# Spreading VectorE's four folds of a batch's values over four half steps

## The chip, the cores and the metric

The kernel runs on one core of a Trainium2 chip. Its time is the device time of one execution in microseconds (us); shorter is better. The core has five engines with one instruction queue each, which run in program order and wait for one another through semaphores: TensorE (PE in the profile, with its weight loads as PEld), VectorE (DVE), ScalarE (ACT), GpSimd (POOL) and SyncE (SP), which here only issues transfers.

## The reference

Attention over pooled keys and values, then a mixture of experts in which every token goes to one expert. The change lies in the pooling of `v`.

```
# q, k, v: (8 batches, 8 heads, 576 tokens, 64)
k_p = k.reshape(B, H, 72, 8, D).mean(axis=3)
v_p = v.reshape(B, H, 72, 8, D).mean(axis=3)
scores = scale * np.matmul(q, k_p.transpose(0, 1, 3, 2))
attn = softmax(scores)
x = np.matmul(attn, v_p)              # to (4608 tokens, 512)
...
logits = x @ w_gate                   # 8 experts
e_idx = np.argmax(logits, axis=1)
out[mask] = gate_w * sigmoid(x @ w_output_gate)[e] * (relu(x[mask] @ w1[e]) @ w2[e])
```

## The kernel before

The program has two parts. `attention_and_routing` does the attention and writes each token's row, sorted by expert, to a table in memory; `experts` then multiplies the sorted rows. The change lies in the first part, whose order is written out by hand.

The 4608 tokens are 36 tiles of 128. The main loop runs over tiles `i` and, within a tile, over two halves of the heads, `a` = 0 (three heads in `values`) and 1 (five). One pass is called a **half step** here and numbered `i` or `i + 0.5`. In half step `i + 0.5 a` the program emits, in this order: TensorE's `scores` of tile `i` (L276); `transpose_p` of tile `i - 2` (L300, evacuated by ScalarE at L301); VectorE's `peak` of tile `i` (L282, the maximum `m`); two units of queued work; TensorE's `values` of tile `i - 3` (L310) with a reciprocal on VectorE (L327); one unit of queued work; ScalarE's `softmax` of tile `i` (L288); VectorE's `normalise` of tile `i - 3` (L333, which empties the accumulator into `xg`); one unit of queued work. There is one accumulator `p_y[a]` for each half of the heads, so `values` of the next tile must wait until `normalise` has emptied it.

The queued work is a list of generators. `work(n)` takes the first whose hold has run out and advances it by one `yield`; the number yielded is the hold in half steps. Two kinds stand there. `route(g)`, appended for each group of four tiles, is some 15 small VectorE operations (L349 to L398) that choose the expert and end in `where`, the table rows, after which GpSimd scatters the group's four tiles (L441). `pooled(b)`, inserted at the head, is the four **folds** (L228) of batch `b`.

Pooling a batch's values goes in stages. SyncE loads `v` of a batch into `vt` (L189), five chunks of 128 rows, one buffer for all batches. GpSimd halves each chunk (L224; `halve_v(b, 0)` is chunks 0 to 2, `halve_v(b, 1)` chunks 3 and 4). VectorE folds what is left twice for each part: **fold 1** (128x384) and **fold 2** (128x192, into the tile `vp`) for chunks 0 to 2, which need the first three halvings, then **fold 3** (128x256) and **fold 4** (128x128, into `vp`) for chunks 3 and 4. `turn_v` (L248) transposes `vp` on TensorE, and `place_v` copies it on ScalarE. `vt` may be loaded again only after the last fold.

A plan says what is emitted at the end of which half step: what stands at `at(s, ...)` is emitted at the end of half step `s + 0.5`. Batch `b` is first used by the scores of half step `f`: 4.5, 9, 13.5, 18, 22.5, 27 and 31.5 for `b` = 1 to 7. Before, the halvings come at the ends of half steps `f - 2.5` and `f - 2`, the four folds all in half step `f - 1`, and at the end of half step `f` come `turn_v` of the batch and the next batch's load of `v`. GpSimd also pools the keys (L202, nine operations a batch).

Of the kernel before, what the change touches and what calls it, by code (L numbers as in the profile page):

```python
# [91 lines left out]
def attention_and_routing(ctx, tc, sh, qT, kT, v, wg, wst, xs):  # L92
# [133 lines left out]
    def pool_v(b, a, n):  # L226
        to = vt[:, part_v(a), 0:n] if n > D else pooled_rows(b)[:, part_v(a)]
        nc.vector.tensor_tensor(to, vt[:, part_v(a), 0:n], vt[:, part_v(a), n:2 * n], op=ALU.add)  # L228
# [293 lines left out]
    plan, queue = {}, []  # L522

    def at(step, f, *args):
        plan.setdefault(step, []).append((f, args))

    def pooled(b):
        for a in range(2):
            for n in (2 * D, D):
                pool_v(b, a, n)  # L530
                yield 0

    tick = [0]

# [14 lines left out]
    for b in range(1, B):  # L549
        f = S * b // P + 0.5 * (b % 2)  # L550
        at(f - 8.5, load_k, b)
        at(max(f - 5, 0), load_v, b)
        at(f - 4.5, load_q, b)
        for i, part in enumerate([(w, c, c + 1) for c in range(4) for w in (4, 2)] + [(1, 0, 4)]):
            step = f - 5.5 + 0.5 * (i // 2)
            at(step if step != -0.5 else 0, pool_k, b, nc.gpsimd, *part)
        at(max(f - 2.5, 1.5), scale_k, b)
        at(f - 3, halve_v, b, 0)
        at(f - 2.5, halve_v, b, 1)
        at(f - 2, lambda b: queue.insert(0, [pooled(b), 0, -1]), b)  # L560
        for c in range(3):
            at(f - 0.5 + 0.5 * c, place_v, b, c)
        at(f - 0.5, turn_v, b)
        at(f + 1.5, gate_v, b)
# [809 lines left out]
def program():  # L1374
# [12 lines left out]
    with ExitStack() as st:  # L1387
# [31 lines left out]
        with tile.TileContext(nc) as tc:  # L1419
            with ExitStack() as ctx, tc.manual_schedule():  # L1420
                attention_and_routing(ctx, tc, sh, qT, kT, v, wg, wst, xs)
# [32 lines left out]
```

## Time and profile before

| what | value |
|---|---|
| median of 3 runs | 602.16 us (602.12 to 604.27) |
| profiled execution, its own time | 602.74 us |
| profiled execution, span of its instructions | 600.8 us |
| TensorE busy | 572.1 us, 95% of the span |
| VectorE, ScalarE, GpSimd busy | 363.7, 256.4 and 223.9 us |

The profile is one execution; its span leaves out 1.94 us around the instructions. Times of rows count from the span's start. Attention fills about the first 150 us, the experts the rest.

### The profile page before, as it was taken

To read this page: it belongs to the slowest core of one execution; us is meant where nothing else is said; L and a number is where in the kernel's file an instruction comes from. 1 tells how busy PE (TensorE), PEld (TensorE's weight loads), DVE (VectorE), ACT (ScalarE), POOL (GpSimd) and SP (SyncE) were. 2 spreads that over 40 slices of the span, in tenths; PEclk is the share of its full clock that TensorE was granted. 3 is DMA by queue.
4 is the path that set the end of the run, shared out by engine and by line. 5 is a ranking of instruction groups with operands and counts; after the bars stand their busy time and mean duration, and the time that the engine had idled before them with its cause. 6 is when DMAs were issued, how large, how long until landed. Compare 5 with 4: busy or idle time off the path is not lost.

```text
span 600.8 us, 11852 instructions
## 1 busy us (share of the span) xinstructions
PE 572.1 (95%) x3427; PEld 518.9 (86%) x3428; DVE 363.7 (61%) x892; ACT 256.4 (43%) x709; POOL 223.9 (37%) x331
## 2 busy tenths in 40 slices
PE   2899999999999999999999999999999999999996
PEld 2798898888888989898989898898998898989895
DVE  6788899988978725698575324664253832232323
ACT  2888988788525304266344121441140430202120
POOL 2849789851526322224224131232202422213131
PEclk9999999999999999999999999999999999999999
DMA  9767888975557433589656213363033112010111
GB/s 338 292 239 289 351 304 314 373 292 163 189 203 193 164 101 116 146 238 327 207 192 202 62 38 88 124 211 64 37 133 99 48 31 69 17 52 19 35 36 35
DMA packets 44683, 96.60 MB, mean 161 GB/s; under 512 B 5515, under 2 KB 28475, under 8 KB 41664
## 3 DMA queue, kind: packets, MB, share of 16 engines
q1 hardware_dynamic: 29328, 48.95, 25.4%
q10 hardware_dynamic: 7488, 27.27, 13.6%
q0 software_dynamic: 7792, 19.61, 9.2%
q14 instruction: 56, 0.46, 0.2%
q8 instruction: 19, 0.31, 0.2%
HBM read 76.36 MB, written 22.91 MB: 165 GB/s over the span
## 4 chain that ended last, share of the span: by engine, by line
PE 68%; issue 2%; DVEq 0%; DVE 0%; POOL 0%; POOLq 0%
PE p_h L1031 34%; PE p_y L1012 33%; PE p_y L665 1%; POOL out L1353 0%; DVE rows L1204 0%; DVEq L1207 0%; PE p_y L1068 0%; DVE q_even L1230 0%; DVEq L793 0%; POOLq L1318 0%; DVEq L767 0%; DVEq L1237 0%; DVEq L926 0%; DVEq L853 0%; DVEq L785 0%
## 5 line engine op out<-in xcount | busy, mean ns | idle before, releaser
L1113 ACT ACTIVATE ht<-p_h 128x384 fp32r<-128x384 f32 (+1 forms) x104 | 46.8, 450 | 246.4 <-PE p_h L1031 219.1
L1353 POOL DMA_INDIRECT out<-rows,dst x41 | 42.2, 1030 | 210.4 <-DVE rows L1204 207.3
L1031 PE MATMUL p_h<-xt,w1b 128*128 128x384 f32 (+1 forms) x736 | 115.5, 317 | 2.0 <-issue 2.0
L1031 PEld LDWEIGHTS p_h<-xt,w1b 128*128 128x128 f32 x736 | 114.4, 189 | 3.3 <-issue 2.9
L1215 DVE SCALAR_TENSOR_TENSOR ht<-p_h,ht 128x384 fp32r<-128x384 f32 (+1 forms) x104 | 52.3, 504 | 100.0 <-ACT ht L1113 90.6
L1012 PE MATMUL p_y<-w2b,ht 128*128 128x512 f32 x480 | 110.4, 390 | 0.0
L1012 PEld LDWEIGHTS p_y<-w2b,ht 128*128 128x128 f32 x480 | 89.8, 188 | 18.4
L1031 PEld LDWEIGHTS p_h<-xt,w1a 128*128 128x128 f32 x640 | 92.7, 190 | 2.6 <-DVE q_even L1230 1.2
L1031 PE MATMUL p_h<-xt,w1a 128*128 128x256 f32 (+1 forms) x640 | 93.7, 306 | 1.2 <-DVE q_even L1230 1.0
L1012 PE MATMUL p_y<-w2a,ht 128*128 128x512 f32 x408 | 94.0, 390 | 0.0
L1012 PEld LDWEIGHTS p_y<-w2a,ht 128*128 128x128 f32 x408 | 76.3, 188 | 15.6
L1204 DVE TENSOR_SCALAR rows<-p_y,sc 128x512 f32<-128x512 f32 x41 | 30.1, 742 | 84.3 <-PE p_y L1012 75.9
L288 ACT ACTIVATE p<-p_h,m 128x72 f32<-128x72 f32 x288 | 69.8, 347 | 16.3 <-DVE m L282 14.3
L310 PE MATMUL p_y<-vbd,pT 128*128 128x162 f32 (+3 forms) x400 | 68.7, 320 | 6.1 <-DVE xg L333 4.4
L1328 POOL DMA_INDIRECT rows<-xs,src x51 | 57.6, 1129 | 25.0 <-POOL src L1324 13.5
L310 PEld LDWEIGHTS p_y<-vbd,pT 128*128 128x128 f32 (+1 forms) x400 | 54.2, 179 | 11.1 <-issue 5.7
L441 POOL DMA_INDIRECT xs<-xg,where x36 | 36.0, 1000 | 38.4 <-DVE grec L327 17.2
L202 POOL TENSOR_TENSOR kq<-kq 128x288 f32<-128x288 f32 (+1 forms) x63 | 42.2, 675 | 17.4 <-DMA kq<-kT 14.4
L276 PE MATMUL p_h<-kbd,q_even 128*128 128x144 f32 (+1 forms) x160 | 28.7, 307 | 11.5 <-DMA q_even<-qT 8.8
L333 DVE TENSOR_TENSOR xg<-p_y,grec 128x240 f32<-128x240 f32 x72 | 35.2, 489 | 1.4
L276 PEld LDWEIGHTS p_h<-kbd,q_even 128*128 128x128 f32 (+1 forms) x160 | 22.8, 191 | 13.6 <-issue 9.5
L1168 DVE STREAM_TRANSPOSE turned<-rows 128x512 f32<-128x512 f32 x51 | 32.4, 686 | 3.2 <-DMA rows<-xs 1.5
(170 smaller groups left out, 657.7 us busy)
## 6 DMA issues: line engine op xcount, KB each, us to landing
stage<-wst ACTq DMA_DIRECT2D x52, 512.0 KB
rows<-v SPq DMA_DIRECT2D x8, 1280.0 KB
kq<-kT SPq DMA_DIRECT2D x7, 1152.0 KB
rows<-xs SPq DMA_DIRECT2D x36, 192.0 KB
stage<-wst SPq DMA_DIRECT2D x12, 512.0 KB, 5.0
kq<-qT SPq DMA_DIRECT2D x4, 1152.0 KB
q_even<-qT SPq DMA_DIRECT2D x3, 1152.0 KB, 8.5
rows<-xs SPq DMA_DIRECT2D x20, 128.0 KB
```

What stands on the lines that cost most here:

```text
L202: eng.tensor_tensor(k[:, :, 0:w], k[:, :, 0:w], k[:, :, w:2 * w], op=ALU.add)
L276: nc.tensor.matmul(s[r0:r0 + n, 144 * c:144 * c + 144], q_t[b][:, 2 * a + c, s0:s0 + n], kbd[b % 2][:, 2 * a + c, :], start=True, stop=True)
L288: nc.scalar.activation(pt[i % 3][:, o:o + KEYS], sv[:, h], AF.Exp, bias=m[:, h:h + 1])
L310: nc.tensor.matmul(av[r0:r0 + n, COLS * h:COLS * (h + n_heads)], pT[:, c, r0:r0 + n], vbd[b % 2][:, slot:slot + n_heads].rearrange("p h f ...
L333: nc.vector.tensor_tensor(xg[g][:, j, 0:LEAD + DM].rearrange("p (f h) -> p f h", h=H)[:, :, hs], avv[:, :, 0:GATE + D].rearrange("p h f -> ...
L441: ins = nc.gpsimd.indirect_dma_start(out=whole_rows(xs), out_offset=bass.IndirectOffsetOnAxis(ap=where, axis=0), in_=x.bitcast(I32), in_of ...
L1012: i = mm(to, ht[:, h, f, P * k:P * k + P], w[:, part, o:o + DM], start=(f == 0 and part == 0 and h == 0), stop=(f == 7 and h == 1))
L1031: i = mm(to, w[:, part, o:o + P], x, start=(d == 0 and k == 0), stop=(d == 3 and k == len(terms) - 1))
L1113: act(ht[:, 0, f, 0:size * P], p_h[f % DEEP][:, 0:size * P], AF.Relu).then_inc(q["hh"], 1)
L1215: nc.vector.scalar_tensor_tensor(ht[:, 1, f, 0:n], src, 0.0, ht[:, 0, f, 0:n].bitcast(F32), op0=ALU.max, op1=ALU.subtract).then_inc(q["hl" ...
L1328: nc.gpsimd.indirect_dma_start(out=xm[:, k].bitcast(I32), out_offset=None, in_=xs, in_offset=bass.IndirectOffsetOnAxis(ap=src[:, k:k + 1], ...
L1353: nc.gpsimd.indirect_dma_start(out=out, out_offset=bass.IndirectOffsetOnAxis(ap=dst[:, k:k + 1], axis=0), in_=yb[2 if k == size - 1 else k ...
```

## The change

`pooled(b)` yields a hold of 1 where it yielded 0, so that at most one fold is taken in a half step, and it is put into the queue half a step sooner. Fold 1 moves from half step `f - 1` to `f - 1.5`, fold 2 stays in `f - 1`, fold 3 moves to `f - 0.5` and fold 4 to `f`. The number of instructions on VectorE and what each computes stay as they are.

```diff
     def pooled(b):
         for a in range(2):
             for n in (2 * D, D):
                 pool_v(b, a, n)
-                yield 0
+                yield 1
...
         at(f - 3, halve_v, b, 0)
         at(f - 2.5, halve_v, b, 1)
-        at(f - 2, lambda b: queue.insert(0, [pooled(b), 0, -1]), b)
+        at(f - 2.5, lambda b: queue.insert(0, [pooled(b), 0, -1]), b)
```

VectorE's rows around the folds of batch 1, in the program before (`m_0` and `m_1` are the maxima of a tile's two halves; L228 with `rows` as output is fold 1 or 3, with `vp` fold 2 or 4):

```order
53 L282 TENSOR_REDUCE m_0_287<-p_h 128x4
54 L327 RECIPROCAL grec_293<-p_y 128x3
55 L333 TENSOR_TENSOR xg_291<-p_y,grec_293 128x80x3
56 L282 TENSOR_REDUCE m_1_307<-p_h 128x4
57 L228 TENSOR_TENSOR rows<-rows 128x3x128
58 L228 TENSOR_TENSOR vp_310<-rows 128x192
59 L327 RECIPROCAL grec_293<-p_y 128x5
60 L228 TENSOR_TENSOR rows<-rows 128x2x128
61 L333 TENSOR_TENSOR xg_291<-p_y,grec_293 128x80x5
62 L228 TENSOR_TENSOR vp_310<-rows 128x128
63 L282 TENSOR_REDUCE m_0_333<-p_h 128x4
```

The four folds stand between two maxima. In the changed program the same stretch begins with fold 1 ahead of the first reciprocal:

```order
53 L282 TENSOR_REDUCE m_0_287<-p_h 128x4
54 L228 TENSOR_TENSOR rows<-rows 128x3x128
55 L327 RECIPROCAL grec_294<-p_y 128x3
56 L333 TENSOR_TENSOR xg_292<-p_y,grec_294 128x80x3
57 L282 TENSOR_REDUCE m_1_308<-p_h 128x4
58 L228 TENSOR_TENSOR vp_310<-rows 128x192
59 L327 RECIPROCAL grec_294<-p_y 128x5
60 L333 TENSOR_TENSOR xg_292<-p_y,grec_294 128x80x5
```

and goes on with folds 3 and 4:

```order
61 L282 TENSOR_REDUCE m_0_331<-p_h 128x4
62 L228 TENSOR_TENSOR rows<-rows 128x2x128
63 L327 RECIPROCAL grec_294<-p_y 128x3
64 L333 TENSOR_TENSOR xg_292<-p_y,grec_294 128x80x3
65 L282 TENSOR_REDUCE m_1_353<-p_h 128x4
66 L228 TENSOR_TENSOR vp_310<-rows 128x128
67 L327 RECIPROCAL grec_294<-p_y 128x5
```

Each fold now stands right behind a maximum; fold 4 is two maxima later than it was. On TensorE the transposes of batch 1's `vp` stand where they stood, and the second of them waits for VectorE (the number behind an engine's name names its semaphore). The rows of the changed program, behind the last `values` of half step 4.5:

```order
47 L310 MATMUL p_y<-vbd_69,pT_282 128x162 [waits DVE_49,Activation_49]
48 L310 MATMUL p_y<-vbd_69,pT_282 128x243
49 L310 MATMUL p_y<-vbd_69,pT_282 128x162
50 L248 MATMUL vtr_367<-ident,vp_310 128x128 [waits PE_49]
51 L248 MATMUL vtr_367<-ident,vp_310 128x128 [waits DVE_49]
52 L248 MATMUL vtr_367<-ident,vp_310 64x128
```

These read the same before; what moved is the fold that row 51 waits for. On GpSimd the scatters of a group move with the routing that shares the queue with the folds. Around the halvings of batch 3, the program before (`where_580` is of group 0, `where_838` of group 1):

```order
69 L441 DMA xs<-xg_291,where_580 39296x528
70 L202 TENSOR_TENSOR kq<-kq 128x4x72 [waits Pool_49]
71 L322 IOTA xg_719 128x4x16
72 L224 TENSOR_TENSOR rows<-rows 128x256 [waits DMAHW6_49]
73 L224 TENSOR_TENSOR rows<-rows 128x256 x4
74 L202 TENSOR_TENSOR kq<-kq 128x288 [waits DMAHW0_49,Activation_49]
75 L202 TENSOR_TENSOR kq<-kq 128x144 [waits Pool_49]
76 L441 DMA xs<-xg_489,where_838 39296x528 [waits DVE_49]
```

and the changed program (`where_603` is of group 0, `where_820` of group 1):

```order
69 L202 TENSOR_TENSOR kq<-kq 128x4x72 [waits Pool_49]
70 L322 IOTA xg_717 128x4x16
71 L441 DMA xs<-xg_292,where_603 39296x528
72 L224 TENSOR_TENSOR rows<-rows 128x256 [waits DMAHW6_49]
73 L224 TENSOR_TENSOR rows<-rows 128x256 x4
74 L441 DMA xs<-xg_489,where_820 39296x528 [waits DVE_49]
75 L202 TENSOR_TENSOR kq<-kq 128x288 [waits DMAHW0_49,Activation_49]
76 L202 TENSOR_TENSOR kq<-kq 128x144 [waits Pool_49]
```

Group 1's first scatter, and VectorE's routing that it waits for, now stand ahead of two of batch 4's key operations instead of behind them.

## Rows read from the trace of the kernel before

**Rows 1.** The page's head and its busy times: us, share of the span, instructions.

```profile
span 600.8 us, 11852 instructions
...
PE 572.1 (95%) x3427; PEld 518.9 (86%) x3428; DVE 363.7 (61%) x892; ACT 256.4 (43%) x709; POOL 223.9 (37%) x331
```

**Rows 2.** Stretches in attention and in the experts: busy us of each engine, clock, DMA.

```profile
60.00:80.00 20.00, 19.52 (x151) 18.15 (x152) 17.84 (x72) 17.14 (x69) 14.68 (x20) 1.00 0.76 295
...
300.00:400.00 100.00, 100.00 (x581) 91.47 (x580) 51.55 (x77) 31.86 (x56) 24.23 (x35) 1.00 0.43 127
```

**Rows 3.** TensorE's waits from 15 to 240 us: us in total, times, longest.

```profile
PE p_y L310 <- DVE xg L333: 4.4, 6, 1.5
```

**Rows 4.** VectorE's waits, the same stretch.

```profile
DVE rows L228 <- POOL rows L224: 4.4, 4, 1.6
```

**Rows 5.** VectorE in order of time, batch 1: start, us, instruction [idle before, releaser].

```profile
23.83 1.07 DVE L228 TENSOR_TENSOR rows<-rows 128x384 f32<-128x384 f32 x1 [1.60 <-POOL rows L224]
24.93 0.77 DVE L228 TENSOR_TENSOR vp<-rows 128x192 f32<-128x192 f32 x1
25.63 0.18 DVE L327 RECIPROCAL grec<-p_y 128x5 f32<-128x5 f32 x1
25.73 0.38 DVE L228 TENSOR_TENSOR rows<-rows 128x256 f32<-128x256 f32 x1
...
26.52 0.61 DVE L228 TENSOR_TENSOR vp<-rows 128x128 f32<-128x128 f32 x1
27.05 0.45 DVE L282 TENSOR_REDUCE m<-p_h 128x4 f32<-128x288 f32 x1
27.42 0.16 DVE L327 RECIPROCAL grec<-p_y 128x3 f32<-128x3 f32 x1
...
27.94 0.45 DVE L282 TENSOR_REDUCE m<-p_h 128x4 f32<-128x288 f32 x1
28.30 0.18 DVE L327 RECIPROCAL grec<-p_y 128x5 f32<-128x5 f32 x1
...
29.01 0.45 DVE L282 TENSOR_REDUCE m<-p_h 128x4 f32<-128x288 f32 x1
```

**Rows 6.** TensorE in order of time, batches 1 and 4.

```profile
23.81 0.72 PE L310 MATMUL p_y<-vbd,pT 128*128 128x162 f32 x4
...
26.75 1.20 PE L310 MATMUL p_y<-vbd,pT 128*128 128x162 f32 x6 [1.10 <-DVE xg L333]
27.79 0.49 PE L248 MATMUL vtr<-ident,vp 128*128 128x128 f32 x3
...
75.31 1.13 PE L310 MATMUL p_y<-vbd,pT 128*128 128x162 f32 x6
...
77.57 0.49 PE L248 MATMUL vtr<-ident,vp 128*128 128x128 f32 x3
```

**Rows 7.** GpSimd in order of time, batches 3 and 4.

```profile
54.60 3.77 POOL L224 TENSOR_TENSOR rows<-rows 128x256 f32<-128x256 f32 x5
58.34 1.60 POOL L202 TENSOR_TENSOR kq<-kq 128x288 f32<-128x288 f32 x2
62.44 0.99 POOL L441 DMA_INDIRECT xs<-xg,where  x1 [2.50 <-DVE grec L327]
...
72.06 3.80 POOL L224 TENSOR_TENSOR rows<-rows 128x256 f32<-128x256 f32 x5
```

**Rows 8.** VectorE in order of time: batch 2's fold 1, and around batch 4's.

```profile
40.64 0.54 DVE L228 TENSOR_TENSOR rows<-rows 128x384 f32<-128x384 f32 x1
...
71.76 0.46 DVE L282 TENSOR_REDUCE m<-p_h 128x4 f32<-128x288 f32 x1
...
74.58 0.70 DVE L228 TENSOR_TENSOR rows<-rows 128x384 f32<-128x384 f32 x1
```

**Rows 9.** SyncE's waits: us in total, times, longest.

```profile
SPq L189 <- DVE vp L228: 72.2, 6, 16.4
```

**Rows 10.** A stretch of two us late in attention, columns as in Rows 2.

```profile
122.00:124.00 2.00, 2.00 (x18) 2.00 (x18) 1.97 (x5) 1.96 (x10) 2.00 (x3) 1.00 1.06 429
```

## The prediction

> **What bounds the kernel now.** I read the page's head and busy times first: TensorE is busy for 95% of the span [rows 1]. The stretches come next. In the experts TensorE is busy for all of a hundred us and VectorE for half of them; in attention TensorE still leads with 19.52 of 20, but VectorE has 17.84, ScalarE 17.14 and GpSimd 14.68 [rows 2]. So in attention four engines run nearly full in lockstep, and a late one shows as a gap on TensorE. The experts have no room to take a delay back: what attention loses, the end loses. The third view is TensorE's waits: between 15 and 240 us the largest is for `normalise` (L333) to empty an accumulator, 4.4 us in six waits [rows 3]; batch 1's, 1.10 us, is one of them [rows 6]. VectorE in turn waits before the folds for GpSimd's halvings, 4.4 us in four waits [rows 4]. The chain is therefore: halvings late, fold 1 waits at the head of VectorE's queue, the reciprocal, `normalise` and the next maximum stand behind it, the accumulator stays full, TensorE stops.
>
> No row shows TensorE waiting at `turn_v` (L248): fold 4 is done by then (batch 1: it ends just before 27.05 [rows 5], the transposes start at 27.79 [rows 6]).
>
> **The change, part by part.** No work is added. Two things move. Fold 1 is asked for half a step sooner, while GpSimd's halvings stand where they stood. And fold 4 is done two half steps later, in the half step at whose end TensorE transposes what it writes; fold 4 is now followed at once by its reader.
>
> Batch 1 in full. GpSimd is not touched by the move, so VectorE is released at 23.83 as before [rows 5], but now from half step 3 and not 3.5. From there on, all gaps from rows 5: fold 1 takes 1.10 (23.83 to 24.93), reciprocal and `normalise` of three heads 0.52 (27.42 to 27.94), so `xg` is ready at 25.45. TensorE asked for that accumulator at 23.81 [rows 6]: 1.64 us lost. Maximum 0.36, fold 2 0.70 (24.93 to 25.63), reciprocal and `normalise` of five heads 0.71 (28.30 to 29.01): 27.22. TensorE needs its own 1.84 us from the first `values` to the second (26.75 less 23.81, less the wait of 1.10), so it arrives at 27.29 and does not wait there. Then maximum 0.37, fold 3 0.38, reciprocal and `normalise` 0.52, maximum 0.36, fold 4 0.53 (26.52 to 27.05): 29.38. TensorE is at the transposes 1.04 us after 27.29, at 28.33, and stands there until 29.38. Before, it began them at 27.79: **batch 1 loses 1.6 us**. The old wait of 1.10 is in this: it is not removed but moved to the other accumulator, half as long again, and the wait for fold 4 is new. Queued behind the waiting transposes are the scores of the next half step and all of TensorE after them.
>
> Batch 4, which did not wait before. Its halvings begin at 72.06 and take 0.76 each (3.80 for five) [rows 7], so the third ends at 74.3, just ahead of fold 1 at 74.58 [rows 8]; half a step sooner, fold 1 would stand behind the maximum of 71.76, at 72.1. The 2.2 us between are what a fold 1 in the new place would wait if nothing else moved. Something does: by then TensorE and VectorE are late by 1.6 (batch 1) and some 0.9 (batch 3, below), which puts the slot at 74.6. GpSimd's chain starts at group 1's first scatter, before at 62.44, and needs 9.62 us to the halvings [rows 7]. In the new order the routing ends half a step sooner against the tiles, so with the delays the scatter starts at about 63.2 (my estimate), but one pair of key operations (at most 1.60 [rows 7]) now lies behind it: halvings at about 74.3, the third done at 76.5. Fold 1 waits 1.9 us and takes up to 1.10, then come routing and a `normalise` (about 0.9): 78.5, where TensorE asked at 75.31 plus 2.5: 0.7 lost. From there to the end of fold 4 VectorE has three maxima, two `normalise`, folds 2 to 4 and some routing, 3.6 us by the gaps above: 82.1. TensorE reaches its transposes at 77.57 plus 2.5 plus 0.7, 80.8: 1.3 lost. **Batch 4 loses 2.0 us** and had lost nothing.
>
> The others by these two. Batch 3 is an odd one like batch 1, but its halvings hang on routing, so TensorE's delay of 1.6 reaches them too: I take the move of the wait at nothing and fold 4 at 0.9. Batch 2 has its halvings early and its VectorE idle: nothing. Batches 5 to 7 come when TensorE is 4.5 us late and GpSimd, whose scatters for groups 1 and 2 come sooner in the order, is less late: its halvings meet the new slots, the old waits go (3.3 us in five waits are left in rows 3 besides batch 1's, of which 1.5 are batch 3's by my share), and fold 4 costs 0.4 to 1.2 each time. I take -0.4, -0.2 and +0.5. Bounds for a fold 4 that isn't in the trace in this place: nothing, if VectorE has caught up with TensorE in three half steps; 1.6, as batch 1, if it has not.
>
> Not on the path: the next load of `v`. SyncE stands before it until the last fold of the batch, 72.2 us in six waits [rows 9], with the loads of `q` and `k` queued behind. Fold 4 is 2 us later or more (27.05 against 29.38 in batch 1), so all of these start later by that. They are hidden by the steps between load and use as long as the transfer engines are not full.
>
> A rule bears on the folds. Fold 1 takes 0.54 us in batch 2, where GpSimd is idle, and 1.07 in batch 1, where it is in the middle of halving [rows 5, 8]. The Trainium skill, "SBUF — State Buffer", "Who interferes with whom", says that a VectorE instruction with two inputs in SBUF contends with a GpSimd instruction that reads SBUF, and that the second to issue is blocked until the first is done. By that rule the folds, one by one among GpSimd's work, would each be held up; that is the third rival.
>
> **The sum.** 1.6 + 0 + 0.9 + 2.0 - 0.4 - 0.2 + 0.5 = 4.4 us. The profiled execution took 602.74 us, 600.8 of it the span; with 4.4 more it would take 607.1. It lies 0.6 above the median of 602.16, so the median becomes 606.5.
>
> **The rivals.** First, on the other side: the smoothing works. If GpSimd has its third halving done before every new slot, VectorE never takes more than one fold between two maxima, and both the 4.4 us of rows 3 and the new wait are gone: 602.16 - 4.4 = 597.8. It decides at the point where the halvings end 1.5 us or more earlier against the maxima than now. For it: scatters of some groups do move forward. Against it: even in the later slot fold 1 or 3 waited in four of seven batches [rows 4], and in batch 4 it missed the wait by 0.3 us [rows 7, 8].
>
> Second: the waits only change places. VectorE catches up before fold 4, so the transposes find it done, and each batch pays what it paid, plus the 0.5 us by which batch 1's second `normalise` is later (27.29 against 26.75), in three or four batches: 602.16 + 2.0 = 604.2. For it: VectorE needs 1.96 us for a whole tile without folds or routing (27.05 to 29.01 [rows 5]) and TensorE at least 2.88 (23.81 to 27.79 less the wait [rows 6]), so it takes back 0.9 us with each tile. Against it: fold 4 and its reader are half a step apart at most, with a maximum between that itself needs TensorE.
>
> Third, the held-up folds: the four gaps of batch 1's folds (1.10, 0.70, 0.38, 0.53) against 0.54 for an unhindered fold 1 bound what all four can lose to GpSimd at some 1.8 us a batch, and about half of that is lost already. Another 0.9 for seven batches is 6.3 us of VectorE, and if half of it reaches TensorE, 3 us more: 609.6.
>
> Fourth, the loads: late in attention the transfer engines are full (429 GB/s, share 1.06 of the time [rows 10]), and a `v` that starts 2 us later or more may land late. Then GpSimd's halvings of batches 6 and 7 slip, and with them TensorE, by up to 2 us each: 610.5.
>
> **Chances and range.** The forecast 0.45, the smoothing 0.06, the mere exchange of waits 0.32, the held-up folds 0.10, the loads 0.07. The predicted time is that of the likeliest, 606.5, with a range of its own from 604 to 609 by the bounds of fold 4 (nothing, or 0.5 more in each of five batches). The overall range leaves out the smoothing and most of the loads, and reaches down to where the exchange of waits costs nothing: 601.8 to 610.3. A measurement can tell about 0.5%, 3.0 us, from no change. Above 605.2 lie nine tenths of the forecast, a little of the second, and the two last: 0.60. Within 0.5%: 0.34. Faster: 0.06.
>
> **What would show it.** Right: TensorE has waits at L248 for VectorE's L228, longest in batches 1, 3 and 4, together 3 to 6 us; VectorE's waits for the halvings rise from 4.4 to 5 us or more, with batch 4 among them; the waits at `values` move from the five heads to the three; the experts' stretches are as long as before and begin 4 us later. Wrong: no L248 among TensorE's waits (then fold 4 is in time), or VectorE's waits for L224 gone (then the halvings are earlier than I put them); SyncE or GpSimd waiting for `v` to land would speak for the loads. If the experts' part itself changes in length, the cause is none of these.

## The result

The changed kernel took 610.12 us (median of five runs, 607.97 to 612.31), the kernel before 602.17 us beside it: a ratio of 1.0120, 95% interval 1.0089 to 1.0152. It is slower, by 8.0 us here. The same kernel timed again among the experiments gave 607.3 us against 602.55, a ratio of 1.0094 (1.0069 to 1.0120). The loss is therefore about 1%, and the two intervals meet at 0.9 to 1.2%.

The profiled run took 610.23 us. Its page, first the head, the busy times and the granted clock of TensorE in 40 slices:

```profile
span 608.5 us, 11860 instructions
...
PE 576.4 (95%) x3427; PEld 522.6 (86%) x3428; DVE 364.7 (60%) x892; ACT 258.5 (42%) x709; POOL 223.3 (37%) x331
...
PEclk9899989999998999999999999999999999999999
```

Against [rows 1] the span has grown by 7.7 us and VectorE has one us more to do; TensorE's busy time has grown by 4.3 us although it does the same work. The 8s in the clock's line say why, and they come back below. TensorE's waits from 15 to 240 us (total, times, longest):

```profile
PE vtr L248 <- DVE vp L228: 5.1, 4, 2.0
PE p_y L310 <- DVE xg L333: 2.5, 2, 1.6
PE p_y L665 <- PEq L1419: 1.9, 1, 1.9
...
PE vtr L248 <- DVE m L282: 0.6, 1, 0.6
```

and the rows that answer to [rows 4], VectorE's, and to [rows 9], SyncE's over the whole span:

```profile
DVE rows L228 <- POOL rows L224: 6.1, 3, 3.6
...
SPq L189 <- DVE vp L228: 93.9, 7, 17.3
```

The wait at the transposes (L248), of which [rows 3] knew nothing, has 5.7 us in five. The wait for the accumulator fell from the 4.4 us of [rows 3] to 2.5, that for the halvings rose from the 4.4 of [rows 4] to 6.1, and the loads of `v` stand longer. In order of time on TensorE:

```profile
25.57 1.03 PE L310 MATMUL p_y<-vbd,pT 128*128 128x162 f32 x4 [1.63 <-DVE xg L333]
...
60.02 0.82 PE L310 MATMUL p_y<-vbd,pT 128*128 128x162 f32 x4 [0.88 <-DVE xg L333]
...
64.27 0.44 PE L248 MATMUL vtr<-ident,vp 128*128 128x128 f32 x2 [1.24 <-DVE vp L228]
...
82.97 0.44 PE L248 MATMUL vtr<-ident,vp 128*128 128x128 f32 x2 [2.02 <-DVE vp L228]
...
119.71 0.44 PE L248 MATMUL vtr<-ident,vp 128*128 128x128 f32 x2 [1.25 <-DVE vp L228]
```

The waits at `values` are at the three heads' accumulator now (x4), where [rows 6] had them at the five heads' (x6); batches 3, 4 and 6 stand at the transposes. At its first layer (L659), where attention hands over, TensorE is 6.2 us late: 159.9 us against 153.7.

A second thing shows in the stretches of two us: busy us of TensorE, its granted clock, the transfers' share, GB/s.

```profile
26.00:28.00 2.00, 2.00 (x13) 0.50 0.06 12
28.00:30.00 2.00, 2.00 (x11) 0.65 0.17 31
...
84.00:86.00 2.00, 2.00 (x9) 0.50 0.93 307
86.00:88.00 2.00, 2.00 (x12) 0.64 1.03 336
...
184.00:186.00 2.00, 2.00 (x6) 0.50 0.96 385
```

Three times the clock was granted at half, 1.2 and not 2.4 GHz, for some 3.4 us each, every time behind a stand of TensorE: 1.63 us in batch 1, 2.02 in batch 4, 1.86 at the hand-over to the experts.

### The profile page after: what moved, and what is told of

Same layout as the page of the kernel before. It is cut to its first block, busy times and chain, and to the rows that moved or that the text cites. A ratio compares the mean times of both kernels' runs of the same rounds, so it can differ in the third digit from the quotient of the medians.

```text
span 608.5 us, 11860 instructions
## 1 busy us (share of the span) xinstructions
PE 576.4 (95%) x3427; PEld 522.6 (86%) x3428; DVE 364.7 (60%) x892; ACT 258.5 (42%) x709; POOL 223.3 (37%) x331
## 4 chain that ended last, share of the span: by engine, by line
PE 66%; issue 2%; DVE 1%; DVEq 0%; ACT 0%; POOL 0%; POOLq 0%
PE p_h L1031 33%; PE p_y L1012 31%; PE p_y L665 2%; ACT w2b L1102 0%; DVE q_even L1230 0%; POOL out L1353 0%; DVE rows L1204 0%; DVE ht L1215 0%; DVE xt L1164 0%; DVEq L1207 0%; DVEq L1163 0%; ACT ht L1121 0%; DVEq L793 0%; DVE w2b L1192 0%; DVEq L1244 0%
## 5 line engine op out<-in xcount | busy, mean ns | idle before, releaser
L310 PE MATMUL p_y<-vbd,pT 128*128 128x162 f32 (+3 forms) x400 | 70.5, 324 | 4.4 <-DVE xg L333 2.5
L310 PEld LDWEIGHTS p_y<-vbd,pT 128*128 128x128 f32 (+1 forms) x400 | 55.9, 184 | 9.2 <-issue 2.3
L282 DVE TENSOR_REDUCE m<-p_h 128x4 f32<-128x288 f32 x72 | 32.5, 451 | 5.6 <-PE p_h L276 3.3
```

The source lines that it names most:

```text
L310: nc.tensor.matmul(av[r0:r0 + n, COLS * h:COLS * (h + n_heads)], pT[:, c, r0:r0 + n], vbd[b % 2][:, slot:slot + n_heads].rearrange("p h f ...
```

## The experiments

The theory after the result: (a) fold 1, half a step sooner, stands before a halving that isn't done, and everything on VectorE behind it; (b) fold 4, in the half step at whose end it is read, is late for the transposes; (c) the clock falls behind some of the stands add to it. The rivals: the spreading itself costs, since it pushes routing and `normalise` back; or the later loads of `v` do.

**Folds two by two, from the old place.** Neither the early start nor one fold to a half step: folds 1 and 2 in one half step, 3 and 4 in the next.

```diff
-                yield 1
+                yield 0 if n > D else 1
-        at(f - 2.5, lambda b: queue.insert(0, [pooled(b), 0, -1]), b)
+        at(f - 2, lambda b: queue.insert(0, [pooled(b), 0, -1]), b)
```

> Folds begun where the kernel before begins them, but two in a half step and the other two in the next (half steps f - 1 and f - 0.5). Main theory (the change loses by fold 1 asking for the halvings half a step too soon and by fold 4 standing right ahead of TensorE's transposes of it): fold 1 is back in its old place and fold 4 half a step ahead of its reader, so TensorE waits less than 1 us in all at L248, VectorE waits some 4.4 us for L224 as before, no fall of the clock, 601 to 604 us. Rival (the spreading itself costs, because routing is pushed back in the queue): about half of the loss stays, 605 to 607.

Measured: 604.62 us, ratio 1.0028 (1.0009 to 1.0047). At L248 0.6 us in two waits, at the accumulator 2.0, for the halvings 2.4. Most of the loss is gone with the two things that were taken out; a quarter of a per cent stays, above what was expected.

**Only the early start.** All four folds in one half step, as before, but half a step sooner.

```diff
-                yield 1
+                yield 0
```

> All four folds in one half step, as before, but half a step sooner (f - 1.5). Main theory: no wait at L248, but VectorE's wait for the halvings grows above 6.1 us because fold 3 asks for the last two halvings sooner too; TensorE's waits at the accumulators grow above 4.4 us and the clock falls at one or two of them: 605 to 611 us. Rival (only the spreading costs): 601 to 603.

Measured: 610.97 us, ratio 1.0139 (1.0112 to 1.0167). TensorE's and VectorE's waits:

```profile
PE p_y L310 <- DVE xg L333: 9.8, 5, 2.4
...
DVE rows L228 <- POOL rows L224: 11.9, 7, 2.6
```

The early start alone, without the spread, costs as much as the whole change: six of the seven batches now wait for their halvings, and the wait goes on to the accumulator. So (a) can carry the loss by itself, and spreading isn't needed for it. Falls of the clock are in this price: the trace has two, behind stands at the accumulator, and all four runs have a mean clock of 0.994 or less. TensorE waits longer at the accumulator here than in the changed kernel, 9.8 us against 2.5, since four folds at once hold up `normalise` longer than one; whether the spread takes time back in this way isn't shown, as the intervals of the two ratios overlap.

**The reader half a step later.** The changed kernel, with `turn_v` at f instead of f - 0.5.

```diff
-        at(f - 0.5, turn_v, b)
+        at(f, turn_v, b)
```

> The changed kernel with the transposes of the folded values (turn_v, L248) half a step later, so that fold 4 is half a step ahead of its reader. Main theory: the 5.7 us of waits at L248 go, and the fall of the clock at batch 4 with them (1.6 us); batch 1's wait at the three-head accumulator and its fall of the clock stay: 602.5 to 605 us. Rival (the late loads of v or the pushed back routing cost): 608 to 611 as the changed kernel.

Measured: 605.67 us, ratio 1.0049 (1.0027 to 1.0072). The wait at L248 is down to 0.3 us, though fold 4 still takes up to 1.62 us; VectorE's wait for the halvings is 7.6 us. TensorE's waits:

```profile
PE p_y L310 <- DVE xg L333: 2.9, 4, 1.2
PE p_y L665 <- PEq L1419: 1.6, 1, 1.6
PE p_y L310 <- DVE running L386: 1.3, 1, 1.3
PE vg L257 <- DVE running L386: 1.2, 1, 1.2
```

That removes about half of the loss: (b). It's 0.7 us over what was expected; two waits for the routing (L386), 2.5 us, have come up, which no theory had named. Batch 1's fall of the clock, which was expected to stay, isn't in this trace.

**The halvings half a step sooner**, in the changed kernel.

```diff
-        at(f - 3, halve_v, b, 0)
-        at(f - 2.5, halve_v, b, 1)
+        at(f - 3.5, halve_v, b, 0)
+        at(f - 3, halve_v, b, 1)
```

> The changed kernel with GpSimd's halvings half a step sooner in its queue. Main theory: VectorE's 6.1 us of waits for L224 shrink in batches 3 and 4 by up to 1 us each, not in batch 1, where the keys' operations still stand ahead; fold 4 comes a little sooner, waits at L248 shrink: 606 to 610 us. If GpSimd's queue were free all the while, nothing changes: 610.

Measured: 609.86 us, ratio 1.0115 (1.0088 to 1.0141). The trace is of the quickest of the five runs, 605.43 us at a clock of 0.998; the other four took 609.42 to 611.32 at 0.993 to 0.997. In it the wait for the halvings is down to 3.6 us and that at the accumulator to 1.2, but L248 is up to 7.8 us in six. Curing (a) alone in this way gives nothing that can be told while (b) stands (the changed kernel's own quickest run, below, took 605.42): VectorE, freed sooner, is still late for the transposes.

**The old folds with the reader right behind them.** The kernel before, with `turn_v` at f - 1.5.

```diff
-        at(f - 0.5, turn_v, b)
+        at(f - 1.5, turn_v, b)
```

> The kernel before, with its four folds in one half step as they were, but the transposes of the batch's values called for one half step after them (f - 1.5) instead of one and a half later. Nothing is spread and nothing begins sooner; only the reader stands right behind the last fold. Main theory (the time goes into the wait of the transposes for the last fold): waits of 1 to 3 us at L248 in several batches, together 4 to 12 us, and 606 to 612 us. Rival (it goes into the early start of the folds or into the pushed-back routing and loads): none of that is here, so little at L248 and 601 to 604 us.

Measured: 621.69 us, ratio 1.0317 (1.0287 to 1.0347), ten us over the main theory's own upper end. TensorE's waits:

```profile
PE vtr L248 <- DVE vp L228: 9.0, 9, 2.4
PE vtr L248 <- DVE grec L327: 7.4, 5, 2.3
```

A reader right behind the last fold is by itself enough to lose, with nothing spread and nothing sooner: 16.4 us of waits in all seven batches. The mechanism was right and the price that was expected for it half of what it was. Part of the price is the clock: in this trace it stands at half for 3.4, 6.8 and 3.4 us, behind stands at L248.

**The changed kernel again**, unaltered, for a second trace.

> The changed kernel once more, unaltered, for a second trace. If the falls of the granted clock in batch 1, in batch 4 and at the hand-over to the experts belong to the change, they stand at the same places again, at half the clock for 3 to 4 us each, and the span is 607 to 610 us. If they come by chance, one or more is missing and the span is shorter by about 1.5 us for each, 604 to 607 us. The waits at L248 are 4 to 7 us in either case.

Measured: 605.42 us in one run. Span, clock and waits:

```profile
span 603.6 us, 11860 instructions
...
PEclk9999999999999999999999999999999999999999
```

```profile
PE vtr L248 <- DVE vp L228: 6.3, 6, 2.0
PE p_y L310 <- DVE xg L333: 2.1, 2, 1.2
```

and batch 4's transposes, with the stretch behind them:

```profile
82.63 0.44 PE L248 MATMUL vtr<-ident,vp 128*128 128x128 f32 x2 [2.03 <-DVE vp L228]
```

```profile
84.00:86.00 2.00, 2.00 (x17) 1.00 0.82 297
```

The same waits at the same places, and no fall of the clock at all: behind a stand of 2.03 us at the transposes the clock stays at 2.4 GHz, where it had halved behind 2.02. The three falls do not belong to these places of the changed kernel.

**The changed kernel, five rounds.**

> The changed kernel once more, unaltered, timed in five rounds. Its times so far are 605.4 with a mean granted clock of 1.000 and 608 to 612.3 with clocks of 0.989 to 1.000. If the falls of the clock make the spread, the time goes down by about 1.5 us for each 0.003 of clock, and the median lies at 606 to 610 us. If 605.4 was a chance and something else makes 608 to 612, the times do not go with the clock and the median is 609 us or more.

Measured: 607.3 us (605.65 to 610.99, six runs), ratio 1.0094. With these there are twelve runs of the changed kernel. Six have a mean clock of 0.998 or more, with a median of 606.8 us (605.42 to 609.42); six have 0.997 or less, with a median of 610.2 (607.97 to 612.31). The time goes with the clock: the two groups' means, 610.2 and 607.0 us, are 3.3 us apart, and their mean clocks, 0.9940 and 0.9993, would by themselves make 3.2 of it (estimate: 0.0053 of 607 us). But it doesn't go wholly with it: one run at a clock of 1.000 took 609.42, and it has no trace. A low clock is not the changed kernel's alone, but it is more frequent there: of 74 runs of the kernel before, timed among the experiments, ten have 0.997 or less (median 604.7 us, 602.5 for the others).

**Folds and reader half a step later.** This was to leave out the early start alone.

```diff
-        at(f - 2.5, lambda b: queue.insert(0, [pooled(b), 0, -1]), b)
+        at(f - 2, lambda b: queue.insert(0, [pooled(b), 0, -1]), b)
-        at(f - 0.5, turn_v, b)
+        at(f, turn_v, b)
```

> The changed kernel with its four single folds and the transposes both half a step later: the folds still one by one, the last still right ahead of the transposes, but the first no longer sooner than it was. What it leaves out of the change is the early start alone. Main theory (half of the loss is the early fold 1, which stands before a halving that is not done, half the transposes behind fold 4): VectorE's waits for the halvings go back to 2 to 4.5 us, the waits at the three heads' accumulator to under 1 us, the waits at L248 stay at 3 to 6 us: 604 to 608 us. Rival (the spread itself is the cost, through routing pushed back and loads of the values): at least as slow as the changed kernel, 608 to 612 us.

Measured: 675.89 us. The kernel was not the one meant: the next batch's `load_v` is called for at the end of the half step before fold 4's, so fold 4 stands behind that load and folds the next batch's values in place of its own. VectorE's row of batch 1:

```profile
35.09 0.29 DVE L228 TENSOR_TENSOR vp<-rows 128x128 f32<-128x128 f32 x1 [6.12 <-DMA rows<-v]
```

It says nothing on the question, and its successor moves the load with the folds.

**The same with its load.** As above, and `load_v` half a step later too.

```diff
-        at(max(f - 5, 0), load_v, b)
+        at(max(f - 4.5, 0), load_v, b)
```

> Folds one by one, fold 4 right ahead of the transposes, fold 1 no sooner than it was: the folds, the transposes and the loads of the values are all half a step later than in the changed kernel, so that a load is again called for behind the last fold of the batch before. It leaves out of the change the early start alone; the halvings stay. Main theory: VectorE's waits for the halvings go back to 2 to 5 us, the waits at the three heads' accumulator to under 1 us, the waits at L248 stay at 3 to 6 us: 603.5 to 607 us. Rival (spreading and later loads are the cost): the loads land later, GpSimd waits 4 us or more for the values, and the time is that of the changed kernel or above, 607 to 612 us.

Measured: 604.04 us, ratio 1.0029 (1.0014 to 1.0044). Waits of TensorE and VectorE:

```profile
PE vtr L248 <- DVE vp L228: 8.5, 6, 2.0
...
DVE rows L228 <- POOL rows L224: 2.3, 2, 1.3
```

Without the early start the waits for the accumulator are gone, and two thirds of the loss with them, though the folds are as spread and the loads of `v` start later still. Both rivals fall as the main cost: spreading and late loads can carry no more than the 0.3% or so that is left. The transposes wait longer than in the changed kernel, 8.5 us, and yet the experts begin at 156.3 us against 157.1 and 157.4 in the changed kernel's traces without a fall: a wait at L248 that takes the place of one at the accumulator is paid once. The trace is of one of the slower runs, 605.64 us.

**Folds 3 and 4 together.** The changed kernel with its fold 4 half a step sooner; the early start stays.

```diff
-                yield 1
+                yield 0 if (a, n) == (1, 2 * D) else 1
```

> The changed kernel with folds 3 and 4 in one half step, so that fold 4 is done half a step sooner and the transposes, where they stand, have half a step more. The early start of fold 1 stays. Main theory: the waits at L248 go to under 1.5 us, those at the accumulator stay at 2 to 5 us, those for the halvings at 5 to 8 us: 603 to 606.5 us, like the kernel with the transposes half a step later (605.67). Rival (the wait at L248 is only where VectorE's lateness shows, and shows elsewhere when fold 4 moves): 608 us or more.

Measured: 605.0 us, ratio 1.0045 (1.0029 to 1.0060). No wait at L248, the halvings 8.8 us in four. TensorE's:

```profile
PE p_y L310 <- DVE xg L333: 3.0, 3, 1.2
PE p_y L310 <- DVE running L386: 2.2, 1, 2.2
```

Half of the loss is gone, as with the later reader, by the opposite edit: it's the distance between fold 4 and its reader that counts.

**All three together.** Two by two from the old place, the reader at f, the halvings half a step sooner (the edits above).

> Folds two by two from the old half step, the transposes half a step later, and the halvings half a step sooner: each wait that the traces name (the fold for its halving, the transposes for the fold) has half a step more. Main theory: no wait at L248, under 1 us of VectorE's waits for the halvings, the waits at the accumulator down to 2 us: 599 to 602 us. Rival (the spread itself costs, by routing and loads that are pushed back): 604 to 607 us.

Measured: 602.56 us, ratio 0.9997 (0.9981 to 1.0014). No wait at L248, 1.2 us at the accumulator, 2.1 for the halvings, and yet no gain: a wait of 1.4 us for ScalarE's `vT` (at L373) has come up, the clock falls right behind it, and ten of the twelve runs have a mean clock of 0.997 or less. It is 0.6 us over what the main theory gave it, and well under its rival.

**The kernel before with the halvings half a step sooner.**

> The kernel before with the halvings alone half a step sooner. If the 4.4 us that VectorE waits for them are what makes TensorE wait 4.4 us for the accumulator, both shrink to 1 us or less and the time is 598 to 601 us. If the halvings are held up by GpSimd's own work and by the landing of the values, they come no sooner: 601 to 604 us.

Measured: 601.2 us, ratio 0.9967 (0.9951 to 0.9983). The waits for the halvings fell from 4.4 to 3.5 us, those at the accumulator from 4.4 to 2.6. It's the only kernel here that is faster than the one before, by 0.3%. Between the two expectations, as the halvings are: batch 4's begin at 71.84 us against 72.06, those of batch 6 in the same place but in one piece, and only batch 7's come clearly sooner, at 119.26 against 121.58.

Side by side, with the waits of the profiled run in us and the start of TensorE's first layer (the medians are of all runs, falls of the clock included):

| kernel | median us | ratio | at L248 | accumulator | halvings | L659 begins |
|---|---|---|---|---|---|---|
| before | 602.17 | 1 | 0 | 4.4 | 4.4 | 153.7 |
| changed | 610.12 | 1.0120 | 5.7 | 2.5 | 6.1 | 159.9 |
| changed, again | 605.42 | one run | 6.3 | 2.1 | 5.8 | 157.1 |
| changed, five rounds | 607.3 | 1.0094 | 5.6 | 1.7 | 4.9 | 157.4 |
| early start alone | 610.97 | 1.0139 | 0 | 9.8 | 11.9 | 161.3 |
| changed, halvings sooner | 609.86 | 1.0115 | 7.8 | 1.2 | 3.6 | 157.4 |
| changed, reader later | 605.67 | 1.0049 | 0.3 | 2.9 | 7.6 | 155.5 |
| changed, folds 3 and 4 together | 605.0 | 1.0045 | 0 | 3.0 | 8.8 | 155.3 |
| changed, without the early start | 604.04 | 1.0029 | 8.5 | 0 | 2.3 | 156.3 |
| two by two from the old place | 604.62 | 1.0028 | 0.6 | 2.0 | 2.4 | 154.0 |
| all three together | 602.56 | 0.9997 | 0 | 1.2 | 2.1 | 153.9 |
| before, halvings sooner | 601.2 | 0.9967 | 0 | 2.6 | 3.5 | 151.8 |

## Why the prediction was right, and where its sizes were off

The way and the mechanism came as forecast; the size didn't quite. 606.5 us were forecast, 610.12 measured: 8.0 us more than before where the sum had 4.4. That is 1.1 us above the range of the likeliest case (604 to 609) and only 0.2 us inside the overall range, so that it lies inside is in part luck. The second set, 607.3, lies in both.

**The bound and the mechanism.** Right. Attention's loss reaches the end: L659 is 6.2 us later and the span 7.7 longer. The three signs that the prediction named are there: waits at L248, 5.7 us where it said 3 to 6; more waiting for the halvings, 6.1 where it said 5 or more, batch 4 among them; the accumulator's waits at the three heads and not the five. Two details differ. In the first trace batch 1 has no wait at L248 and batch 6 has 1.25 us; the second has 0.53 in batch 1. And the experts, which were to be as long as before, took 1.5 us more in the first trace (L659 to the end, 448.6 us against 447.1), which the prediction named as a sign of another cause; the second trace and that of the five rounds have 446.5. That cause is the clock, below.

The experiments show the two steps as causes: without the early start the ratio is 1.0029, with fold 4 and its reader further apart 1.0045 or 1.0049, against 1.0094 to 1.0120. Runs at a mean clock of 0.998 or more, taken by themselves, keep the order: medians of 602.5 us before, 606.8 changed (six runs), 605.65 with the reader later (seven), 605.0 with folds 3 and 4 together (four), 603.7 without the early start (nine). There the change costs 4.3 us; the early start takes 3.1 of them with it, the distance between fold 4 and its reader 1.2 or 1.8. They need not be two terms of a sum: a VectorE that is held at fold 1 is also later at fold 4, and where only one of the two waits is left, the next tiles take some of it back.

**The sum by batches.** The delay that each batch adds, read at its `gate_v` (L257) against the kernel before, in us:

| batch | forecast | first trace | second trace |
|---|---|---|---|
| 1 | 1.6 | 2.07 | 1.52 |
| 2 | 0 | 0.09 | 0.32 |
| 3 | 0.9 | 0.85 | 0.83 |
| 4 | 2.0 | 4.01 | 2.34 |
| 5 | -0.4 | -0.29 | -0.45 |
| 6 | -0.2 | 0.82 | 0.25 |
| 7 | 0.5 | -1.35 | -1.41 |
| sum | 4.4 | 6.20 | 3.40 |

The rows of batch 4's `gate_v`, in the kernel before and in the changed kernel's first trace:

```profile
83.99 0.90 PE L257 MATMUL vg<-wgd,vT 128*128 128x64 f32 x6
...
91.01 0.90 PE L257 MATMUL vg<-wgd,vT 128*128 128x64 f32 x6
```

The second trace, without falls of the clock, follows the forecast within 0.5 us in six of seven batches. Batch 1 came close: fold 4 was forecast to be done at 29.38, and in the second trace the transposes that wait for it go on at 29.36. Batch 4's total is right partly by luck: fold 1 waited 0.7 us and not 1.9, and the accumulator wasn't waited for at all where 0.7 had been put; but fold 4 was done at 82.92 in the first trace, not 82.1, and the transposes stood 2.02 us, not 1.3. Batch 7 was wrong in sign: it was to lose another wait, and it gained. In the kernel before it has four waits of 0.20 to 0.30 us between 128 and 137 us, two for the accumulator and two for ScalarE's `pT`, 1.1 us together; in the second trace one of 0.54, at the transposes, stands in their place. That is 0.5 of the 1.4 us; the rest is in shorter gaps.

**What the sum left out.** The falls of the clock, in the first trace, and they are the step that failed in size: the sum has no term for them. Batch 1: from the first `values` to the transposes TensorE took 4.29 us (25.57 to 29.86), where its own work is 2.88 by [rows 6], so 1.41 lost, and slowed so far that fold 4 was done in time and L248 didn't wait. Batch 4: 8.04 us from the transposes to L257 (82.97 to 91.01) against 6.37 in the second trace (82.63 to 89.00), 1.67 lost. At the hand-over:

```profile
182.60 9.36 PE L665 MATMUL p_y<-w2a,ht 128*128 128x512 f32 x33 [1.86 <-PEq L1419]
```

and in the trace of the five rounds

```profile
179.54 7.74 PE L665 MATMUL p_y<-w2a,ht 128*128 128x512 f32 x33 [1.56 <-PEq L1419]
```

The same 33 matmuls took 7.74 us there: 1.62 lost. Together 4.7 us of the first trace's 610.23, which leaves 605.5; the second trace has 605.42 and that of the five rounds 605.65. That this fits so closely is in part luck: of batch 1's 1.41 us only 0.55 is left at its L257 (2.07 against 1.52), since the slow clock spared it the wait for fold 4. The forecast of 606.5 lies above the two traces without a fall, beside the median of the six runs at a clock of 0.998 or more (606.8), and below the median of all, to which the clock belongs.

**The rival of the held-up folds** was right for fold 4 and wrong for the folds together. It put what a batch can lose at 1.8 us, but the rows of the kernel before give 1.25 (batch 1's four folds 2.83 us, batch 2's 1.58). It expected 6.3 us more of VectorE in all. The 28 folds took 16.4 us before, and 17.0, 19.0 and 16.4 in the three traces of the changed kernel: the hold-up grew by 0.6, 2.6 and 0.0 us. It moved, from fold 2 (5.05 us in seven batches before, 2.7 in the first trace) to fold 4 (2.3 and 5.2), and there the reader stands right behind it. Fold 4 of batch 1 had been put at 0.53 us. Batch 4's, with GpSimd beside it:

```profile
80.97 0.96 POOL L441 DMA_INDIRECT xs<-xg,where  x1 [0.31 <-issue]
...
81.42 1.50 DVE L228 TENSOR_TENSOR vp<-rows 128x128 f32<-128x128 f32 x1
...
81.96 0.80 POOL L202 TENSOR_TENSOR kq<-kq 128x288 f32<-128x288 f32 x1
```

It ends at 82.92, 0.16 us behind the key operation, which ends at 82.76; an unhindered fold 4 takes 0.28 (batch 2). Batch 6's ends as far behind its key operation (118.69 and 0.80, so 119.49; the fold 118.26 and 1.39, so 119.65). These two look as if the fold stood until the key operation was all but done. The Trainium skill, "SBUF — State Buffer", "Who interferes with whom", which the prediction cites, says that a VectorE instruction with two inputs in SBUF contends with a GpSimd instruction that reads SBUF, and that issue order decides who blocks. These two rows agree with it but for the order, since the fold has the earlier start by 0.54 and 0.43 us. Batch 3's fold 4 does not look so:

```profile
62.93 0.98 POOL L441 DMA_INDIRECT xs<-xg,where  x1 [2.93 <-DVE where L398]
63.26 0.96 DVE L228 TENSOR_TENSOR vp<-rows 128x128 f32<-128x128 f32 x1
63.95 0.92 POOL L202 TENSOR_TENSOR kq<-kq 128x288 f32<-128x288 f32 x1
```

It ended at 64.22, 0.31 us behind the scatter and 0.65 ahead of the key operation, which took 0.12 us longer than the other two. What part the scatter has in either was not tried apart. Fold 4 took 5.2 us in seven batches, 3.3 more than seven times 0.28. It is not the whole of the wait at L248: without the early start seven folds took 2.7 us, and the transposes waited 8.5. There VectorE was late by what stood ahead of fold 4: maxima, `normalise`, routing and in batch 3 a held-up fold 3 (1.10 us).

**The other rivals.** The smoothing did not come: the halvings were no earlier than the new slots, and even where they were called for half a step sooner the median did not fall clear of the noise (1.0115). The mere exchange of waits is near the quickest runs (605.42, forecast 604.2) but not the median. The loads: GpSimd waited 2.2 us for the `v` of batch 2, and that batch added 0.09 us; with loads later still the time was 604.04.

**Open.** What decides whether the clock falls behind a stand, since the same stand had it once and once not; the runs at a full clock that took 607.69 and 609.42; why the kernel with all three repairs, whose waits are among the shortest, has a low clock in ten of twelve runs; and why the four kernels at 1.0028 to 1.0049 stay above the kernel before, beyond the waits for routing (L386) that the traces of two of them show.

## What to carry to other kernels

Before work is spread over steps, look at both ends of the chain: the first piece must not be asked for before its input is there, since an in-order queue holds everything behind it, and the last must stay some way ahead of its reader. The slack that a block of work has behind it is part of the schedule, even when it looks idle in the trace. A sum of waits is no price: one kernel here waited 8.5 us at the transposes and came to the experts only 2.6 us later, because another wait had gone; read the delay at a common instruction further down.

## What the runs showed of the hardware that was not expected

A stand of TensorE can cost more than its length. Behind stands of 1.63, 2.02 and 1.86 us the granted clock fell to 1.2 GHz for some 3.4 us, and 1.4 to 1.7 us were lost each time; behind stands of 2.03 us (second trace) and 1.71 us (the hand-over without the early start) it did not fall. In the trace of the early start alone two stands of the same length differ: behind the first the clock stayed, behind the second it fell.

```profile
60.28 0.82 PE L310 MATMUL p_y<-vbd,pT 128*128 128x162 f32 x4 [1.77 <-DVE xg L333]
134.46 1.24 PE L310 MATMUL p_y<-vbd,pT 128*128 128x162 f32 x4 [1.77 <-DVE xg L333]
```

Of the folds that began while a scatter was under way, those that were held up by more than 0.1 us, 23 in the traces here (without the kernel of 675.89 us), all had a key operation or a halving of GpSimd behind that scatter, and none another scatter. It doesn't hold the other way: without the early start batch 4's fold 4 began 0.3 us into a scatter with a key operation behind it and took 0.28. In the second trace two folds (3 and 4 of batch 5) each began half a us into a scatter:

```profile
96.54 0.96 POOL L441 DMA_INDIRECT xs<-xg,where  x1 [0.30 <-issue]
97.11 0.42 DVE L228 TENSOR_TENSOR rows<-rows 128x256 f32<-128x256 f32 x1
97.80 0.96 POOL L441 DMA_INDIRECT xs<-xg,where  x1 [0.30 <-issue]
98.34 1.41 DVE L228 TENSOR_TENSOR vp<-rows 128x128 f32<-128x128 f32 x1
98.79 1.36 POOL L202 TENSOR_TENSOR kq<-kq 128x288 f32<-128x288 f32 x2
```

The first, with another scatter behind, took 0.42 us for twice the columns; the second, with a key operation behind, took 1.41. GpSimd's spans in a profile are rough, and the cause of the early hold was not tried.
